# Attention, softplus layer and bilinear layer on one core: four entries of a hand-written order changed

## The chip, the core and the metric

The kernel runs as one program on one core of a Trainium2 chip. The metric is the device time of one execution in microseconds (us); the number that counts is the median of several executions. Within the core, TensorE (PE) multiplies matrices, VectorE (DVE), ScalarE (ACT) and GpSimd (POOL) work element by element, and SyncE (SP) issues the DMA transfers. Each engine works through a queue of its own, in order.

## The reference

The reference chains three parts over 3072 tokens of width 512, all in float32.

```
# 1: attention in chunks of 32 queries; each sees 56 keys around it and 8 memory keys
scores = scale * q_c @ k_full.T ; a = softmax(scores) ; x = a @ v_full
# 2: 512 -> 2048 -> 512
h = x @ w_in ;  g = maximum(h, 0) + log1p(exp(-abs(h))) ;  x = g @ w_out
# 3: 512 -> 1536 -> 512
out = ((x @ w_a) * (x @ w_b)) @ w_out2
```

## The kernel before

Tokens are cut into 8 tiles of 384 (`t` = 0 to 7). Products keep nearly full float32 precision: each operand is split into a rounded high part and a low part (names ending in `h` and `l`, or index 0 and 1), and three matmuls (high times high, high times low, low times high) are summed in PSUM.

**First phase.** For every tile and each of 16 feature blocks `f`, `emit_h` runs 12 matmuls into `ph` (L538), `emit_soft` computes the softplus (ACT: three passes over `e`, L544 to L546; DVE: `g`, L548; ACT rounds `g` to its high part, L525; POOL, or DVE in tile 0 and the last, makes the low part, L528), and `emit_x1` runs 12 matmuls into `px` (L561), two blocks later than the `ph` they come from. At a tile's end four `xo` copies (L569) go out to `x1_scratch` (L570).

**Attention in between.** Attention comes in units of 128 queries, three to a tile, and is worked on while the tile before it is in the first phase. A list `plan` of (slot, step) sets the place of each step; a slot is a half-step, two to each `f`, so `att_at(slot)` is called twice per block. A unit's steps are: turn keys and queries (L410 to L415), scores (matmuls `sc`, L302 to L305 or L429), softmax (L379, L383), normalise (L387 to L390), flip (transpose the weights into `af`), values (matmuls `pxa`, L476, which need `af`), and place (ACT casts the high part of `x`, L483; DVE makes the low part, L484). For the first units, worked on during tile 0, the flip is done on TensorE: `flip_p` runs 8 transposes `pa` (L465) and ACT copies them to `af` (L466). Their slots stand in `EARLY_STEPS`. From tile 1 on DVE does the flip, in two times five transposes (L447). The matmuls `sc`, `pxa` and `pa` share one pair of PSUM banks (tag "att").

**Weights.** In tile 0 the weights of the first phase are still being turned from 64-bit words into two floats: ACT `top` (L116), DVE `value` (L121, L122), ACT `high` (L127), DVE `low` (L130). During tiles 1 to 6 the weights of the last phase get the first half of this treatment (class `Early`): a fetch into `raw` (L625, L628, on SP), `top` on ACT (L635), `value` on DVE (L639, L640) and a store of `val` (L643, on SP). Five weights to a tile; `PRE_BY` is their distance in half-steps and `PRE_STEPS` the offset of the four steps. The fetch of one weight goes into the buffer that the weight before it leaves, so it waits for that weight's L640.

**Last phase.** Tokens are worked on in four pairs of tiles (`p`), with 12 feature blocks each. `pair_step` runs seven sums of six matmuls with 384 columns (L725), multiplies the results on DVE into `c` and splits `c` again (high: L807, L817 on ACT; low: L818 and, deferred through `pair_step.late`, L819 on DVE). After every second block six output jobs are queued; a `job` is six matmuls of 512 columns into `py` (L748), an addition to `y` on DVE (L757) and, in the last group, the transfer of `y` to the output (L760). Three jobs are taken out within each `pair_step`, and what is left is run after the last.

The program is recorded under a manual schedule: in tile 0 and from tile 7 on all engines follow the recorded order, in tiles 1 to 6 SP, PE and DVE do.

Of the kernel before, what the change touches and what calls it, by code (L numbers as in the profile page):

```python
# [23 lines left out]
TURN_LATER = ((STEPS[0][0] + 0.5, "turn"),) + STEPS[1:]  # L24
SETS = 1
EARLY_STEPS = (((4.9, "scores"), (5, "weigh"), (9, "flip_p"), (10.9, "values"), (11, "place")),
               ((12.9, "scores"), (13, "weigh"), (18, "flip_p"), (19.9, "values"), (20, "place")),
               ((20.9, "scores"), (21, "weigh"), (26, "flip_p"), (27.9, "values"), (28, "place")))
EARLY = len(EARLY_STEPS)
NEXT_LATER = 1.5  # L30
# [12 lines left out]
OUT_TAGS = "eegg"  # L43

PRE, PRE_BY = 5, 4.2
PRE_STEPS = (0, 3.4, 4.1, 4.3)
GROUP = 2


# [1 line left out]
def attn_moe_moe2(ctx: ExitStack, tc: tile.TileContext, q, k, v, mem_k, mem_v,  # L51
                  w_in, w_out, w_a, w_b, w_o2, out):
    nc = tc.nc
    B, H, S, D = q.shape
    M = mem_k.shape[2]
    NT, DM = out.shape
    F1 = w_in.shape[1]
    F2 = w_a.shape[1]
    P = 128
# [9 lines left out]
    NTILE = NT // TT  # L69
    KT = DM // P  # L70
    NF1 = F1 // P
    NF2 = F2 // P
# [446 lines left out]
    acc = {}  # L519
# [199 lines left out]
    def product(bank, p, f, n, first_):  # L719
        i, j = PLACE[n]  # L720
        u, x = us[p, f][i], sums[p, n]
        m = 0
        for kt in range(KH):
            for a, c in ((0, 0), (0, 1), (1, 0)):
                nc.tensor.matmul(bank[:, :TT], lhsT=u[:, j, a, kt * P:kt * P + P], rhs=x[:, c, kt, :],  # L725
                                 start=first_ and m == 0, stop=m == 3 * KH - 1, skip_group_check=True)
                m += 1

    def bank(tag, name):
        return ps.tile([P, 512], F32, tag=tag, name=name, bufs=1 if tag.startswith("acc") else 2)  # L730

    def temp(tag, name):
        return mp.tile([P, TT], F32, tag=tag, name=name, bufs=3 if tag in ("gh", "gl") else 2)

    cs, yacc, jobs, n_jobs = {}, {}, [], [0]
    tt = nc.vector.tensor_tensor

    def job(p, m, half, i):

        b = bank(f"acc{1 + n_jobs[0] % 3}", f"py{p}_{m}_{half}{i}")  # L740
        n_jobs[0] += 1
        fs = range(GROUP * m, GROUP * m + GROUP)
        n = 0
        for f in fs:
            c, w = cs[p, f, half], w2o[p, f]
            r = slice(i * P, i * P + P)
            for x, y in ((0, 0), (0, 1), (1, 0)):
                nc.tensor.matmul(b, lhsT=c[:, x, r], rhs=w[:, y], start=n == 0, stop=n == 3 * GROUP - 1)  # L748
                n += 1
        place = 3 * (1 - half) + i  # L750
        if m == 0:
            if place % 2 == 0:
                yacc[p, place // 2] = wp.tile([P, 2, 512], F32, tag="w", name=f"y{p}_{place // 2}")
            nc.scalar.copy(yacc[p, place // 2][:, place % 2], b)
        else:
            y = yacc[p, place // 2][:, place % 2]
            tt(y, b, y, ALU.add)  # L757
            if m == NF2 // GROUP - 1:
                r0 = (2 * p + half) * TT + i * P
                nc.sync.dma_start(out[r0:r0 + P, :], y)  # L760

    def next_job():
        if jobs:
            job(*jobs.pop(0))

    def pair_step(p, f, at, between=()):

        late_lo = pair_step.late
        x = bank("h", f"pX{p}_{f}")
        product(x, p, f, "11", True)  # L770
        s = temp("e", f"s{p}_{f}")
        nc.scalar.copy(s, x[:, :TT])
        at(0)
        y = bank("att", f"pY{p}_{f}")
        product(y, p, f, "s2", True)
        q = temp("gh", f"q{p}_{f}")
        tt(q, y[:, :TT], s, ALU.add)
        while late_lo:
            late_lo.pop(0)()
        at(1)  # L780
        if between:
            between[0]()
        else:
            next_job()
        w = bank("att", f"pW{p}_{f}")
        product(w, p, f, "s3", True)
        r = temp("e", f"r{p}_{f}")
        tt(r, w[:, :TT], q, ALU.add)
        at(2)
        if between:  # L790
            between[1]()
        v = bank("acc0", f"pV{p}_{f}")
        product(v, p, f, "s1", True)
        d22 = temp("gl", f"d22_{p}_{f}")
        tt(d22, v[:, :TT], r, ALU.add)
        at(3)
        if not between:
            next_job()
        product(x, p, f, "12", False)
        at(4)  # L800
        product(w, p, f, "22", False)
        d21 = temp("e", f"d21_{p}_{f}")
        tt(d21, w[:, :TT], q, ALU.add)  # L803
        c2 = temp("gl", f"c2_{p}_{f}")
        tt(c2, d21, d22, ALU.mult)  # L805
        cs[p, f, 1] = cc = wp.tile([P, 2, TT], F32R, tag="w", name=f"c{p}_{f}_1")
        nc.scalar.copy(cc[:, 0], c2)  # L807
        at(5)
        if not between:
            next_job()  # L810
        product(v, p, f, "s4", False)
        d12 = temp("g", f"d12_{p}_{f}")
        tt(d12, v[:, :TT], q, ALU.add)
        c1 = temp("g", f"c1_{p}_{f}")
        tt(c1, x[:, :TT], d12, ALU.mult)  # L815
        cs[p, f, 0] = c = wp.tile([P, 2, TT], F32R, tag="w", name=f"c{p}_{f}_0")
        nc.scalar.copy(c[:, 0], c1)  # L817
        tt(cc[:, 1], c2, cc[:, 0].bitcast(F32), ALU.subtract)  # L818
        late_lo.append(lambda: tt(c[:, 1], c1, c[:, 0].bitcast(F32), ALU.subtract))  # L819
        at(6)  # L820
        if f % GROUP == GROUP - 1:
            jobs.extend((p, f // GROUP, half, i) for half in (1, 0) for i in range(TT // P))
# [3 lines left out]
    def order():  # L826
# [29 lines left out]
        for i in range(BPT + 4):  # L856
            for d, step in ROUND:
                warm(FILL.get((i, step), 0))
                if d is None:
                    n = i - (step == "low")  # L860
# [29 lines left out]
        for n, e in enumerate(pre[:n_pre]):  # L890
            t, i = divmod(n, PRE)
            for d, step in zip(PRE_STEPS, (e.fetch, e.top, e.value, e.store)):
                plan.append((2 * NF1 * (t + 1) + PRE_BY * i + d, 100 + n, step))
# [56 lines left out]
        for p in range(NTILE // 2):  # L950
            more = p + 1 < NTILE // 2
            for f in range(NF2):

                def at(k):
# [22 lines left out]
                    if more:  # L977
# [8 lines left out]
                        if f == NF2 - 1:  # L986
                            if k < 5:
                                split_hi(p + 1, PRODUCTS[k], nc.scalar.copy)
                            if 0 < k < 6:
                                split_lo(p + 1, PRODUCTS[k - 1], nc.gpsimd if k in (2, 4) else nc.vector)  # L990

                pair_step(p, f, at, (between_0, between_0) if (p, f) == (0, 0) else ())
        while jobs:
            if len(jobs) == 3 and pair_step.late:
                pair_step.late.pop()()
            next_job()

    order()


# [28 lines left out]
```

## Time and profile before

| what | before |
|---|---|
| median of 3 executions | 1196.25 us (1195.96 to 1202.92) |
| the profiled execution | 1196.18 us, of which its span is 1194.1 us |
| TensorE busy | 1180.2 us, 99% of the span |
| ScalarE, VectorE, GpSimd busy | 536.3, 736.9 and 279.3 us |
| mean granted TensorE clock | 0.998 of full speed |

The span reaches from the first to the last instruction; the 2.1 us between it and the execution's time lie outside the trace. TensorE's busy time includes matmuls that run at a lower clock, so idle time and granted clock have to be read together.

### The profile page before, as it was taken

How to read it: one execution, taken by the hardware profiler on the slowest of the kernel's cores; microseconds unless marked ns; L12 is line 12 of the kernel's file. 1: busy time of each engine (PE TensorE's matmuls, PEld its weight loads, DVE VectorE, ACT ScalarE, POOL GpSimd, SP SyncE). 2: the span in 40 equal slices, each digit the busy share in tenths (PEclk: the TensorE clock that was granted, in tenths of full speed). 3: DMA queues.
4: the chain of work that ended last, by engine and by line, in shares of the span. 5: the costliest groups of instructions: out<-in, count | busy, mean ns of one | idle time of the engine just before them, and what ended most of it. 6: DMA issues, size and time to landing. Idle time of an engine off the chain costs nothing.

```text
span 1194.1 us, 21573 instructions
## 1 busy us (share of the span) xinstructions
PE 1180.2 (99%) x7994; PEld 1120.6 (94%) x7994; DVE 736.9 (62%) x1706; ACT 536.3 (45%) x1329; POOL 279.3 (23%) x249
## 2 busy tenths in 40 slices
PE   8999999999999999999999999999999999999998
PEld 8899999999999999999999999999999999999997
DVE  7888654556545565455387677755656456655565
ACT  6898656665566666566564433211112211212110
POOL 1000322323223222232325878200211002100000
PEclk9999999999999999999999999999999999999999
DMA  9955244352443534432465895788554965379521
GB/s 238 300 168 107 81 109 101 108 102 86 109 97 111 102 92 103 111 95 66 149 231 208 324 342 199 267 316 308 202 197 142 373 232 182 129 265 364 185 77 54
DMA packets 198697, 209.86 MB, mean 176 GB/s; under 512 B 121616, under 2 KB 149952, under 8 KB 198592
## 3 DMA queue, kind: packets, MB, share of 16 engines
q1 hardware_dynamic: 198208, 208.43, 54.7%
q8 instruction: 63, 1.03, 0.4%
q14 instruction: 42, 0.34, 0.1%
q0 software_dynamic: 384, 0.05, 0.0%
HBM read 158.11 MB, written 50.33 MB: 175 GB/s over the span
## 4 chain that ended last, share of the span: by engine, by line
PE 89%; DVE 3%; ACT 3%; DMA 2%; SPq 1%; issue 1%; DVEq 0%; ACTq 0%
PE ph L538 20%; PE px L561 20%; PE py L748 17%; PE pW L725 8%; PE pV L725 8%; PE pX L725 8%; PE pY L725 4%; PE pxa L476 2%; PE sc L429 1%; DMA kp<-in_k_dram 1%; DVE af L447 1%; DMA raw<-in_moe_w_in_dram 1%; ACT sm L383 1%; SPq L330 1%; DVE g L548 1%
## 5 line engine op out<-in xcount | busy, mean ns | idle before, releaser
L538 PE MATMUL ph<-x,w 128*128 128x384 f32 x1536 | 289.7, 336 | 0.1
L538 PEld LDWEIGHTS ph<-x,w 128*128 128x128 f32 x1536 | 267.0, 188 | 2.4 <-issue 0.3
L748 PE MATMUL py<-w2o,c 128*128 128x512 f32 x864 | 222.9, 394 | 0.7 <-DVE c L818 0.5
L548 DVE SCALAR_TENSOR_TENSOR g<-ph,e 128x384 f32<-128x384 f32 x128 | 71.3, 557 | 206.7 <-ACT e L546 198.8
L748 PEld LDWEIGHTS py<-w2o,c 128*128 128x128 f32 x864 | 159.9, 188 | 26.8 <-DVE c L818 1.1
L807 ACT CAST c<-c 128x384 fp32r<-128x384 f32 x48 | 24.7, 514 | 303.9 <-DVE c L805 271.2
L725 PE MATMUL pX<-x,u 128*128 128x384 f32 x576 | 115.5, 334 | 0.0
L757 DVE TENSOR_TENSOR y<-py,y 128x512 f32<-128x512 f32 x120 | 82.9, 691 | 48.2 <-PE py L748 47.8
L544 ACT ACTIVATE e<-ph 128x384 f32<-128x384 f32 x128 | 62.3, 486 | 102.3 <-PE ph L538 86.5
L725 PEld LDWEIGHTS pX<-x,u 128*128 128x128 f32 x576 | 102.1, 188 | 4.1
L447 DVE STREAM_TRANSPOSE af<-sm 32x256 f32<-32x256 f32 x180 | 78.2, 435 | 2.6
L545 ACT ACTIVATE e<-e 128x384 f32<-128x384 f32 x128 | 67.3, 526 | 4.0
L803 DVE TENSOR_TENSOR d<-pW,q 128x384 f32<-128x384 f32 x48 | 26.7, 557 | 68.4 <-PE pW L725 68.4
L546 ACT ACTIVATE e<-e 128x384 f32<-128x384 f32 x128 | 67.3, 526 | 3.7
L383 ACT ACTIVATE sm<-sm,st 128x96 f32<-128x96 f32 x168 | 60.5, 361 | 4.9 <-DVE st L379 4.9
L817 ACT CAST c<-c 128x384 fp32r<-128x384 f32 x48 | 24.6, 513 | 77.8 <-DVE c L815 76.9
L725 PE MATMUL pW<-xs,u 128*128 128x384 f32 x288 | 57.8, 335 | 0.0
L725 PE MATMUL pV<-xx,u 128*128 128x384 f32 x288 | 57.8, 335 | 0.0
L725 PE MATMUL pW<-xx,u 128*128 128x384 f32 x288 | 57.6, 334 | 0.0
L725 PE MATMUL pY<-xs,u 128*128 128x384 f32 x288 | 57.6, 334 | 0.0
L725 PE MATMUL pV<-xs,u 128*128 128x384 f32 x288 | 57.6, 334 | 0.0
L725 PEld LDWEIGHTS pV<-xx,u 128*128 128x128 f32 x288 | 51.5, 188 | 4.1
(251 smaller groups left out, 2240.0 us busy)
## 6 DMA issues: line engine op xcount, KB each, us to landing
u<-u_scratch SPq DMA_DIRECT2D x108, 512.0 KB
u_scratch<-u SPq DMA_DIRECT2D x36, 512.0 KB
w2o<-w2o_scratch SPq DMA_DIRECT2D x36, 512.0 KB
u<-u_scratch SPq DMA_DIRECT2D x36, 256.0 KB
raw<-in_moe_w_in_dram SPq DMA_DIRECT2D x16, 512.0 KB
raw<-in_moe_w_out_dram SPq DMA_DIRECT2D x16, 512.0 KB
vn<-in_v_dram SPq DMA_DIRECT2D x35, 176.0 KB
raw_a<-in_moe_w_a_dram SPq DMA_DIRECT2D x12, 512.0 KB
```

What stands on the lines that cost most here:

```text
L383: nc.scalar.activation(sm[:, h], sm[:, h], AF.Exp, bias=st[:, 0, h:h + 1], scale=-1.0, accum_out=st[:, 1, h:h + 1])
L447: nc.vector.transpose(out=af[32 * kb:32 * kb + 32, x], in_=self.sm[32 * x:32 * x + 32, :, 32 * kb:32 * kb + 32])
L538: nc.tensor.matmul(ph, lhsT=a, rhs=c, start=n == 0, stop=n == 3 * KT - 1)
L544: nc.scalar.activation(e, ph, AF.Abs)
L545: nc.scalar.activation(e, e, AF.Exp, scale=-1.0)
L546: nc.scalar.activation(e, e, AF.Ln, bias=1.0)
L548: nc.vector.scalar_tensor_tensor(g, ph, 0.0, e, ALU.max, ALU.add)
L561: nc.tensor.matmul(acc[t][i][:, :TT], lhsT=a, rhs=c, start=f == 0 and m == 0, stop=f == NF1 - 1 and m == 2)
L725: nc.tensor.matmul(bank[:, :TT], lhsT=u[:, j, a, kt * P:kt * P + P], rhs=x[:, c, kt, :], start=first_ and m == 0, stop=m == 3 * KH - 1, sk ...
L748: nc.tensor.matmul(b, lhsT=c[:, x, r], rhs=w[:, y], start=n == 0, stop=n == 3 * GROUP - 1)
L757: tt(y, b, y, ALU.add)
L803: tt(d21, w[:, :TT], q, ALU.add)
```

## The change

Four things change. The second entry of `EARLY_STEPS` has `flip_p` in slot 17 instead of 18. `PRE_STEPS` puts the steps `value` and `store` of the last phase's weights 0.9 half-steps later. In the last `pair_step` of all no job is taken out between the sums `pY` and `pW`, so that seven jobs instead of six are left for the end, and the deferred L819 is recorded when five are left instead of three. The very last job is run as two jobs of 256 columns each, with a bank, an addition and a transfer of its own for each.

```
 EARLY_STEPS = (...
-               ((12.9, "scores"), (13, "weigh"), (18, "flip_p"), (19.9, "values"), (20, "place")),
+               ((12.9, "scores"), (13, "weigh"), (17, "flip_p"), (19.9, "values"), (20, "place")),
-PRE_STEPS = (0, 3.4, 4.1, 4.3)
+PRE_STEPS = (0, 3.4, 5, 5.2)
...
-    def job(p, m, half, i):
+    def job(p, m, half, i, cols=slice(0, DM)):
...
-                nc.tensor.matmul(b, lhsT=c[:, x, r], rhs=w[:, y], start=n == 0, stop=n == 3 * GROUP - 1)
+                nc.tensor.matmul(b, lhsT=c[:, x, r], rhs=w[:, y, cols], start=n == 0, stop=n == 3 * GROUP - 1)
...
-                nc.sync.dma_start(out[r0:r0 + P, :], y)
+                nc.sync.dma_start(out[r0:r0 + P, cols], y)
...
-        else:
+        elif (p, f) != (NTILE // 2 - 1, NF2 - 1):
             next_job()
         w = bank("att", f"pW{p}_{f}")
...
         while jobs:
-            if len(jobs) == 3 and pair_step.late:
+            if len(jobs) == 5 and pair_step.late:
                 pair_step.late.pop()()
-            next_job()
+            if len(jobs) == 1:
+                last = jobs.pop()
+                job(*last, cols=slice(0, DM // 2))
+                job(*last, cols=slice(DM // 2, DM))
+            else:
+                next_job()
```

Three places show how the order moves. The first is ScalarE in tile 0, around block 9 of the first phase; `pa_4` are the TensorE transposes of the unit in question, and `raw`, `tmp`, `w` the weights of the first phase. Before:

```order
L116 ACTIVATE raw_1215<-raw_1215 128x512
L544 ACTIVATE e_9_1320<-ph_9_1301 128x384
L545 ACTIVATE e_9_1320<-e_9_1320 128x384
L546 ACTIVATE e_9_1320<-e_9_1320 128x384
L127 CAST w_1326<-tmp_1283 128x512
L525 CAST g_9h<-g_9_1324 128x384
L116 ACTIVATE raw_1217<-raw_1217 128x512
L466 COPY af<-pa_4_1337 96x4x128
L466 COPY af<-pa_4_1343 96x4x128
```

After:

```order
L466 COPY af<-pa_4_1301 96x4x128
L466 COPY af<-pa_4_1307 96x4x128
L116 ACTIVATE raw_1215<-raw_1215 128x512
L544 ACTIVATE e_9_1332<-ph_9_1313 128x384
L545 ACTIVATE e_9_1332<-e_9_1332 128x384
L546 ACTIVATE e_9_1332<-e_9_1332 128x384
L127 CAST w_1338<-tmp_1283 128x512
L525 CAST g_9h<-g_9_1336 128x384
L116 ACTIVATE raw_1217<-raw_1217 128x512
```

The two copies to `af` now stand ahead of block 9's softplus instead of behind it; the rows that follow them (w, `e_10`, raw, `g_10h`, w, and the cast of `x` from `pxa`, L483) are the same as before. On TensorE the 8 transposes stand ahead of `ph_9` instead of behind it, and nothing else moves there in tile 0.

The second place is VectorE early in tile 3, blocks 2 and 3; `af<-sm` are the flips, five transposes each, and `val_b` is a weight of the last phase.

```order
 L548 SCALAR_TENSOR_TENSOR g_2_3697<-ph_2_3680,e_2_3693 128x384
-L639 TENSOR_SCALAR val_b_3720<-raw_b_3598 128x512
-L640 SCALAR_TENSOR_TENSOR val_b_3720<-raw_b_3598,val_b_3720 128x512
 L447 STREAM_TRANSPOSE af<-sm_3612 32x256 x5
-L548 SCALAR_TENSOR_TENSOR g_3_3748<-ph_3_3731,e_3_3744 128x384
+L639 TENSOR_SCALAR val_b_3727<-raw_b_3598 128x512
+L640 SCALAR_TENSOR_TENSOR val_b_3727<-raw_b_3598,val_b_3727 128x512
+L548 SCALAR_TENSOR_TENSOR g_3_3747<-ph_3_3730,e_3_3743 128x384
 L447 STREAM_TRANSPOSE af<-sm_3612 32x256 x5
```

The two instructions of `val_b` now stand behind the first five transposes. The same happens at the start of tile 6 (and in tiles 2, 4 and 5 at this block). In tile 1, block 5, the pair instead moves from ahead of `g_5` to between `g_5` and the low part of `x` (L484).

The third place is TensorE in the last `pair_step` and behind it; `pX`, `pW`, `pV` are its sums, `py_4` and `py_5` jobs of the last two groups. Before:

```order
L748 MATMUL py_4_02_12912<-w2o_8_12500,c_8_0_12634 128x512 x3
L748 MATMUL py_4_02_12912<-w2o_9_12602,c_9_0_12736 128x512 x3
L725 MATMUL pV_11_12877<-xx_11407,u_11_3_12790 128x384 x6
L748 MATMUL py_5_10_12933<-w2o_10_12704,c_10_1_12818 128x512 x3
L748 MATMUL py_5_10_12933<-w2o_11_12806,c_11_1_12910 128x512 x3
```

After:

```order
L748 MATMUL py_4_01_0_12904<-w2o_8_12500,c_8_0_12634 128x512 x3
L748 MATMUL py_4_01_0_12904<-w2o_9_12602,c_9_0_12736 128x512 x3
L725 MATMUL pV_11_12869<-xx_11407,u_11_3_12790 128x384 x6
L748 MATMUL py_4_02_0_12925<-w2o_8_12500,c_8_0_12634 128x512 x3
L748 MATMUL py_4_02_0_12925<-w2o_9_12602,c_9_0_12736 128x512 x3
L748 MATMUL py_5_10_0_12933<-w2o_10_12704,c_10_1_12818 128x512 x3
L748 MATMUL py_5_10_0_12933<-w2o_11_12806,c_11_1_12902 128x512 x3
```

One job that needs nothing from the last block, `py_4_02`, now stands between the last sum `pV` and the first job that needs the last block's `c`. On VectorE L819 now stands behind the addition of the first `py_5` job instead of the third.

## Rows read from the trace of the kernel before

**Rows 1.** The profile's first part: busy us, share of the span, instructions.

```profile
PE 1180.2 (99%) x7994; PEld 1120.6 (94%) x7994; DVE 736.9 (62%) x1706; ACT 536.3 (45%) x1329; POOL 279.3 (23%) x249
```

**Rows 2.** Waits of TensorE, whole span: total us, times, longest.

```profile
PE pxa L476 <- DVE af L447: 1.6, 2, 1.1
```

**Rows 3.** Timeline of tile 0: start, us, engine, line; idle before, and its end.

```profile
87.92 2.25 PE L538 MATMUL ph<-x,w 128*128 128x384 f32 x12
...
89.91 0.51 ACT L525 CAST g_9h<-g 128x384 fp32r<-128x384 f32 x1 [0.42 <-DVE g L548]
...
90.89 1.04 ACT L466 COPY af<-pa 96x512 f32<-96x512 f32 x2
...
91.50 0.33 PE L476 MATMUL pxa<-af,vn 96*64 96x64 f32 x2 [1.34 <-ACT af L466]
...
93.06 0.49 PE L561 MATMUL px<-g_8h,w 128*128 128x384 f32 x1
...
95.53 0.58 ACT L483 CAST x<-pxa 128x512 fp32r<-128x512 f32 x1
...
96.67 0.68 DVE L484 TENSOR_TENSOR x<-pxa,x 128x512 fp32r<-128x512 f32 x1
...
96.91 0.29 PE L304 MATMUL sc<-kn,qn 64*64 64x88 f32 x1
...
97.41 0.29 PE L304 MATMUL sc<-kn,qn 64*64 64x88 f32 x1
```

**Rows 4.** Windows of tile 0: PE, PEld, DVE, ACT, POOL busy, granted clock, DMA.

```profile
93.00:93.50 0.50, 0.50 (x6) 0.44 (x3) 0.18 (x1) 0.47 (x2) 0.00 (x0) 0.82 0.00 0
...
96.50:97.00 0.50, 0.50 (x4) 0.17 (x5) 0.50 (x2) 0.18 (x1) 0.00 (x0) 0.77 0.90 288
```

**Rows 5.** Timeline of tile 1, blocks 5 and 6, three engines.

```profile
147.53 0.53 ACT L546 ACTIVATE e<-e 128x384 f32<-128x384 f32 x1
...
148.26 0.69 DVE L640 SCALAR_TENSOR_TENSOR val_b<-raw_b,val_b 128x512 uint32<-128x512 uint32 x1
148.86 0.55 DVE L548 SCALAR_TENSOR_TENSOR g<-ph,e 128x384 f32<-128x384 f32 x1
149.33 0.68 DVE L484 TENSOR_TENSOR x<-pxa,x 128x512 fp32r<-128x512 f32 x1
...
150.07 0.88 PE L429 MATMUL sc<-kt,qt 64*64 64x96 f32 x28 [0.55 <-DVE x L484]
```

**Rows 6.** Timeline of tile 3, blocks 2 and 3.

```profile
286.30 0.56 DVE L548 SCALAR_TENSOR_TENSOR g<-ph,e 128x384 f32<-128x384 f32 x1 [3.20 <-ACT e L546]
...
288.06 1.05 DVE L640 SCALAR_TENSOR_TENSOR val_b<-raw_b,val_b 128x512 uint32<-128x512 uint32 x1 [0.87 <-ACT raw_b L635]
...
294.16 0.69 PE L476 MATMUL pxa<-af,vn 96*64 96x64 f32 x16 [1.13 <-DVE af L447]
```

**Rows 7.** Timeline of the end: TensorE and the last addition.

```profile
1182.31 7.73 PE L748 MATMUL py<-w2o,c 128*128 128x512 f32 x31 [0.55 <-DVE c L818]
...
1190.08 0.69 DVE L757 TENSOR_TENSOR y<-py,y 128x512 f32<-128x512 f32 x1 [0.67 <-PE py L748]
```

**Rows 8.** Chain that ended last, near the end: start, us, what.

```profile
1177.13 1.04 PE pW L725 x6
1178.17 1.39 PE py L748 x6
```

**Rows 9.** Window at the last output transfer; the last column is GB/s.

```profile
1191.75:1192.00 0.25, 0.00 (x0) 0.00 (x0) 0.00 (x0) 0.00 (x0) 0.00 (x0) 1.00 1.00 385
```

**Rows 10.** Timelines of SP and ACT: fetches of raw weights, and their `top`.

```profile
140.20 0.38 SPq L628 DMA_DIRECT2D raw_b<-in_moe_w_b_dram  x1
...
144.36 0.67 ACT L635 ACTIVATE raw_b<-raw_b 128x512 f32<-128x512 f32 x1
...
289.13 0.33 SPq L625 DMA_DIRECT2D raw_o<-in_moe_w_out_dram  x1
...
295.15 0.68 ACT L635 ACTIVATE raw_o<-raw_o 128x512 f32<-128x512 f32 x1
```

More of the change, by code (lines that the diff above doesn't have):

```diff
@@ L736, in attn_moe_moe2 @@
     tt = nc.vector.tensor_tensor
-    def job(p, m, half, i):
-        b = bank(f"acc{1 + n_jobs[0] % 3}", f"py{p}_{m}_{half}{i}")
+    def job(p, m, half, i, cols=slice(0, DM)):
+        b = bank(f"acc{1 + n_jobs[0] % 3}", f"py{p}_{m}_{half}{i}_{cols.start}")[:, cols]
         n_jobs[0] += 1
@@ L755, in job @@
         else:
-            y = yacc[p, place // 2][:, place % 2]
+            y = yacc[p, place // 2][:, place % 2, cols]
             tt(y, b, y, ALU.add)
```

## The prediction

> **What bounds the kernel now.** I read the parts in this order: busy times, TensorE's waits, then the timelines around each wait. TensorE is busy 1180.2 us of a span of 1194.1 [rows 1], so an edit of the order can win back only part of 13.9 us of idle time, plus what TensorE loses at a lower clock. The list of waits then says where the change can reach: `pxa` waits for the flips on VectorE 1.6 us in all, in two places, the longer one 1.1 [rows 2], so the other is 0.5. The timelines add three more places: `pxa` in tile 0 behind the copies to `af` (1.34 us), `sc` in tile 1 behind the low part of `x` (0.55 us) and the first `py_5` job behind L818 (0.55 us) [rows 3, 5, 7]. Everywhere else in the stretches that the change touches TensorE goes from one block to the next without a gap, so an edit there costs or gains nothing unless it makes a new wait. The clock is the last thing to read: in tile 0 it falls to half inside the window from 93.00 and is back inside the window from 96.50. Shares of 0.82 and 0.77 put the ends at 93.32 and 96.73 [rows 4], so the stretch is 3.4 us long.
>
> **Tile 0, the flip a half-step sooner.** On TensorE the 8 transposes and `ph_9` change places, so `ph_10` still ends at 90.2 (87.92 + 2.25 [rows 3]). `pxa` then finds its `af` copied and starts at once, at about 90.0 instead of 91.50: the wait of 1.34 us goes. The block behind it also runs at full clock, so that TensorE has done `pxa` (1.1 us) and `px` of block 8 (12 matmuls at 173 ns, from 1.04 us for six [rows 8]: 2.1 us) by 93.1, where before it had them at 96.91. Next come the scores of the following unit. Some 0.4 us of them have a bank that is free; the others cannot start before `x` is read out of the shared banks by L484 at 96.67; before, they restarted at 97.41, 0.06 us after it ended [rows 3]. So what decides is when L484 comes, and that is set by ScalarE: L483, on which L484 waits, stands in ScalarE's queue behind block 10's softplus.
>
> How much sooner can L483 come? Between 89.91 and 95.53 ScalarE works through the same instructions as before, less the two copies (1.04 us), but those now stand ahead of `e_9` and push it back. VectorE's `g_9` then waits for `e_9` about 0.65 us longer (it started at about 89.32, as soon as VectorE was free, with `e_9` ready some 0.3 us earlier; `e_9` now comes 0.95 later), and the cast `g_9h`, at 89.91 before, starts at 90.56. From there the missing copies give back 0.95 (the distance at which the next instruction followed them): 0.3 us sooner in all. The bounds: nothing, if everything is pushed back by as much as the copies take; 0.42, the one idle time of ScalarE in front of `g_9h` [rows 3]. I take 0.3, so the scores restart at 97.1 and TensorE stands idle from 93.5 to 97.1, 3.6 us in one piece where it had 1.34 and about 0.1 before.
>
> Now the clock. Before, TensorE fell idle at 90.2, and the clock fell at 93.3, after 1.34 us of idle time and 1.1 us of the small `pxa` matmuls; most of the half-clock stretch lay on `px` of block 8, whose 12 matmuls took 3.85 us instead of 2.08 (from 93.06 to the first scores at 96.91 [rows 3]). That cost nothing, because the scores could start no sooner than L484 allowed. After the change the longer idle time should make the clock fall again, and this time the matmuls behind the wait pay, with nothing to hide them: behind the scores TensorE goes on for tens of microseconds without a wait that could take them up. If the clock falls 3.1 us after the idle time starts, as before, at 96.2, and is back 3.4 us later at 99.6, then 2.5 us of the stretch lie behind 97.1 and cost half of that, 1.2 us. Bounds: 0 (the whole stretch inside the wait) and 1.7 (all 3.4 us behind it). I take 1.2, as the one whose timing a row shows. Sum for tile 0: -0.3 + 1.2 = **+0.9 us**, bounds -0.4 to +1.7.
>
> The Trainium skill, page "TensorE: Matmul & The Clock Gate", section "Why this matters for your kernels", speaks against this edit: it advises against idle gaps between matmul bursts, since the clock goes back to half rate after one. By it the fall is sure and the sum stands; were there none, tile 0 would be -0.3 and the whole 1193.4. The trace has a fall after 1.34 us of idle time in tile 0 and none at the 1.13 us in tile 3.
>
> **VectorE's part of the weights later.** It adds and removes no instruction, only moves L639 and L640, together about 1.1 us.
> - Tile 3. Before, `g` (286.30), L640 (0.87 us of idle time for `top`, then 1.05 us), five transposes, `g`, five transposes, `pxa` [rows 6]. After, the first five transposes fill the time in which VectorE waited for `top`, and the second five end 0.87 us sooner or more, since L640 took 1.05 here and 0.69 where GpSimd was idle [rows 5, 6]: 0.36 more. That is 1.2 against a wait of 1.13. I take **-1.1**, bounds -0.9 and -1.13.
> - Tile 6 has the same rows and a wait of 0.5 [rows 2]: **-0.5**; bounds -0.5 and -0.3, if only part of it was due to the weight.
> - Tile 1. Here the pair moves from ahead of `g_5` to between `g_5` and L484, for which `sc` waits 0.55 us [rows 5]. The two used to run while ScalarE was still on `e_5`; `g_5` can start only when L546 ends, at 148.06, where VectorE, without L639 (0.42) ahead of 148.26, is free at 147.8. So 0.3 us is lost on VectorE in front of L484 and `sc` starts that much later. GpSimd's low part of `g_5` also starts sooner and will overlap L640, which may cost up to the 0.36 of above. **+0.6**, bounds 0 and +0.9.
> - The Trainium skill, page "Advanced Engine Details and Errata", section "GPSIMD Details", says that GpSimd shares a read and a write interface with VectorE and conflicts with its instructions that have two SBUF inputs. L640 has two; by this rule tile 1 would be +0.65, without a conflict +0.3. The trace agrees so far as L640 took 1.05 beside GpSimd's work and 0.69 beside none.
> - Elsewhere the pair moves behind softmax or flips, of which no one waits on L640 but the next fetch (a rival, below). The stores on SP now stand behind eight of the key and query loads, which is a gain for the loads. Cost nothing.
>
> **The end.** The kept job (1.39 us [rows 8]) now covers the wait for L818 (0.55 us [rows 7]), since L818 and what leads to it come 1.39 sooner against the jobs. At the second `py_5` half the 31 matmuls take 7.73 us, where 31 at 232 ns (1.39 / 6) are 7.19: some 0.3 of the 0.54 is lost to the late L819, the rest is the last matmul draining. L819 now comes two additions earlier, 1.4 us, which covers it. The `y` addition behind the kept job goes to VectorE ahead of L819, where there is room. Both together: **-1.0 us**, bounds -0.85 and -1.3.
>
> The last job in halves: no row shows a 256-column matmul. Half of a 512-column one is 116 ns, and it should not take more than the 384-column one, 173. Twelve cost 1.39 to 2.08 us against 1.39 for the six: between 0 and +0.7. I take 120 ns, +0.05, since both longer shapes go by 0.45 ns a column. Behind the last matmul the addition has half the columns (0.69 to about 0.42, from the 0.56 for 384 and 0.69 for 512: -0.27), and the last transfer half of 256 KB, at 385 GB/s [rows 9] 0.34 us less. **-0.55**, bounds -0.6 and +0.1.
>
> **Sum.** +0.9 - 1.1 - 0.5 + 0.6 - 1.0 - 0.55 = -1.65 us, on an execution of 1196.18, which is the median (1196.25) to 0.1 us: **1194.6 us**. With all lower ends it is 1192.5, with all upper ends 1196.9.
>
> **Rivals.** (1) *The clock costs more than all else wins.* The wait in front of the scores is 2.7 times the one before; if the half-clock stretch comes twice in a row (6.8 us, all behind 97.1), tile 0 costs -0.3 + 3.4 = +3.1, and the sum is +0.55: 1196.8, slower than before. It decides from 5.8 us of half clock behind the wait (2.9 us, what the rest wins). For it: the long idle time. Against it: the one fall that the trace shows ended after 3.4 us. (2) *The clock stays up, or its low stretch lies inside the wait.* Then tile 0 gains 0.3, sum -2.85: 1193.4. For it: much of the stretch may fall into 3.6 us of wait. (3) *The weights' transfers come late.* The next fetch waits for L640, which moves by up to 1.7 us (tile 3). There the fetch left at 289.13 and its `top` ran at 295.15; a fetch is known to land within 4.2 us (140.20 to 144.36, where `top` waited for nothing) [rows 10]. After the change the distance is 6.0 - 1.7 - 1.1 = 3.2, so ScalarE may be held up to 1.0 us in front of its softplus. If two tiles pass that on to TensorE, +2.0: 1196.6. Against it: a block's `g` is needed only two blocks later.
>
> **Chances.** The forecast 0.55, rival 1 0.13, rival 2 0.2, rival 3 0.07, others 0.05. The range takes in rivals and bounds, 1192.0 to 1198.6; its upper end leaves 1.7 us above the worst sum because one of the three executions shown lies 6.7 us above the other two. A measurement of this kernel tells a change from none at about 1%, 12 us; no case comes near that, so faster 0.02, same 0.96, slower 0.02.
>
> **What would show it.** Right: no wait of `pxa` for the copies, a wait of some 3.6 us at `sc` L304 behind L484 near 97, a stretch at half clock that starts near it and covers scores and `ph_11`; `pxa` without a wait in tiles 3 and 6; a wait of 0.9 to 1.2 at `sc` in tile 1; the jobs' matmuls at the end without a gap. Wrong: L484 more than half a microsecond sooner, no fall of the clock, a wait of ScalarE for `raw`, or 256-column matmuls at 170 ns.

## The result and the profile after

The changed kernel is slower: 1215.63 us median of six executions (1213.49 to 1218.22) against 1197.66 of six of the kernel before (1195.96 to 1202.92), a ratio of 1.0143 with a 95% interval of 1.0116 to 1.017. That is 17 to 18 us more, where 1.65 us of gain was forecast.

The profiled execution has a span of 1215.4 us, 21.3 us above that of before. Two views show where TensorE spends them. First the page's busy times, then the list of TensorE's waits (total us, times, longest), both of the changed kernel; [rows 1, 2] are the same of before.

```profile
PE 1191.2 (98%) x8000; PEld 1131.8 (93%) x8000; DVE 739.8 (61%) x1707; ACT 538.5 (44%) x1329; POOL 282.8 (23%) x249
```

```profile
PE pxa L476 <- DVE af L447: 11.9, 7, 2.3
PE sc L304 <- DVE x L484: 3.2, 1, 3.2
PE sc L429 <- DVE x L484: 1.9, 3, 0.9
```

Idle time grew from 13.9 to 24.2 us, and busy time by 11.0 us although no more was added than six matmuls (twelve of half width stand for six): the second is a lower clock, in the mean 0.987 of full speed against 0.998. The wait that was to shrink, `pxa` for the flips, went from 1.6 us in two places to 11.9 in seven. To see in which stage the time goes, the next table counts from the first `xo` copy (L569) of one tile to that of the next, in us; its cells are differences of start times read in the two timelines, and of the spans' ends (1194.08 and 1215.44 us).

| stretch | before | after | difference |
|---|---|---|---|
| start to the first `ph` (L538) | 37.41 | 41.87 | +4.5 |
| first `ph` to the first `xo`: tile 0 | 94.24 | 96.18 | +1.9 |
| tile 1 | 74.94 | 77.82 | +2.9 |
| tile 2 | 73.87 | 76.26 | +2.4 |
| tile 3 | 75.72 | 78.37 | +2.7 |
| tile 4 | 73.92 | 77.26 | +3.3 |
| tile 5 | 73.87 | 75.87 | +2.0 |
| tile 6 | 73.62 | 76.90 | +3.3 |
| tile 7 to its first `xo` | 62.87 | 62.86 | 0.0 |
| from there to the end | 553.62 | 552.06 | -1.6 |

The 4.5 us ahead of the first `ph` are not the change's: nothing is moved there, and that stretch took from 37.6 to 42.1 us in the executions of the experiments below. What differs is the clock, which in this execution was at half from 18.4 to 32.1 us. The window around it, in the changed kernel and in the one before (us busy of PE, PEld, DVE, ACT, POOL with counts; granted clock; DMA share; GB/s):

```profile
18.00:33.00 15.00, 15.00 (x147) 13.40 (x145) 10.42 (x45) 11.34 (x39) 0.00 (x0) 0.54 0.99 254
18.00:33.00 15.00, 12.68 (x193) 11.04 (x192) 13.86 (x59) 13.63 (x51) 0.00 (x0) 1.00 1.01 252
```

What is left is 16.5 us in tiles 1 to 6, that is in the weights' part, which the prediction had at -1.0; 1.9 in tile 0 (predicted +0.9); and -1.6 at the end (predicted -1.55).

**One tile closely.** The chain of work through tile 1, in the changed kernel (start, us, what; "issue" is time that waits for nothing that the profile shows):

```profile
168.67 0.40 DVE val_o L639
169.07 0.02 issue
169.10 1.85 DVE val_o L640
170.95 0.02 SPq L628
170.97 0.04 issue
171.01 3.91 DMA raw_a<-in_moe_w_a_dram
174.93 0.02 issue
174.95 0.67 ACT raw_a L635
175.61 0.42 ACT e L546
...
176.12 0.56 DVE g L548
176.68 0.03 issue
176.71 0.04 DVE af L447
```

And the timelines of GpSimd, ScalarE and TensorE there (start, us, engine and line; in brackets the idle time before and what ended it):

```profile
168.90 1.49 POOL L390 TENSOR_TENSOR sm<-sm,st 128x768 f32<-128x768 f32 x1 [4.96 <-ACT e L544]
170.35 1.46 POOL L528 TENSOR_TENSOR g_7l<-g,g_7h 128x384 fp32r<-128x384 f32 x1
...
174.95 0.67 ACT L635 ACTIVATE raw_a<-raw_a 128x512 f32<-128x512 f32 x1 [1.39 <-DMA raw_a<-in_moe_w_a_dram]
...
179.00 0.69 PE L476 MATMUL pxa<-af,vn 96*64 96x64 f32 x16 [1.75 <-DVE af L447]
```

The same place in the kernel before, of which the prediction shows no row (timelines of VectorE, SP and ScalarE; this kernel runs 6.74 us earlier here, by the `g` that starts at 161.14 before and at 167.88 after):

```profile
157.59 0.69 DVE L640 SCALAR_TENSOR_TENSOR val_o<-raw_o,val_o 128x512 uint32<-128x512 uint32 x1
161.14 0.56 DVE L548 SCALAR_TENSOR_TENSOR g<-ph,e 128x384 f32<-128x384 f32 x1 [2.86 <-ACT e L546]
...
168.07 2.24 DVE L447 STREAM_TRANSPOSE af<-sm 32x256 f32<-32x256 f32 x5
...
158.31 0.40 SPq L628 DMA_DIRECT2D raw_a<-in_moe_w_a_dram  x1
...
164.60 0.66 ACT L635 ACTIVATE raw_a<-raw_a 128x512 f32<-128x512 f32 x1
165.77 0.49 ACT L544 ACTIVATE e<-ph 128x384 f32<-128x384 f32 x1 [0.51 <-PE ph L538]
...
166.85 0.53 ACT L546 ACTIVATE e<-e 128x384 f32<-128x384 f32 x1
```

Read downwards: `val_o` is the third of the tile's five weights. Its L640 stood ahead of `g` and the normalise step and now stands behind both: it starts 4.8 us later (169.10 against 157.59 + 6.74) and takes 1.84 us instead of 0.69, while GpSimd's L390 and then L528 run beside it. The fetch of the fourth weight waits for it and leaves 6.0 us later (171.01 against 165.05). The transfer takes 3.9 us, so its `top` can run at 174.95; before, it ran 6.3 us after its fetch left, which means 2.4 us in hand. ScalarE's queue has that `top` between the second and the third pass of softplus `e_9`. So L546 ends 1.9 us late, `g` behind it starts late too, and `g` stands in VectorE's queue ahead of the second five transposes, on which `pxa` waits. Every tile from 1 to 6 has this wait once, of 1.75, 1.58, 1.78, 1.89, 2.06 and 2.28 us.

The place of `top` is not the same in all six. ScalarE does not follow the recorded order in these tiles. In the kernel before, `top` stands ahead of all three passes of `e_9`; in the changed kernel it stands between the second and the third in tiles 1 to 3, and ahead of all three in tiles 4 to 6, where it holds ScalarE for 2.84, 2.85 and 3.11 us. Tile 4:

```profile
404.54 0.67 ACT L635 ACTIVATE raw_a<-raw_a 128x512 f32<-128x512 f32 x1 [2.84 <-DMA raw_a<-in_moe_w_a_dram]
405.11 0.47 ACT L544 ACTIVATE e<-ph 128x384 f32<-128x384 f32 x1
```

**The clock behind the waits.** Windows of the changed kernel, as above:

```profile
330.00:335.00 5.00, 3.22 (x38) 2.93 (x38) 4.85 (x11) 2.87 (x7) 1.00 (x1) 0.74 0.08 21
335.00:340.00 5.00, 5.00 (x54) 4.63 (x54) 1.21 (x3) 1.18 (x2) 1.01 (x1) 0.91 0.95 215
410.00:415.00 5.00, 5.00 (x32) 4.93 (x27) 3.36 (x7) 1.62 (x5) 1.01 (x1) 0.66 0.59 165
560.00:565.00 5.00, 2.72 (x39) 2.28 (x38) 4.53 (x10) 2.75 (x6) 1.00 (x1) 0.96 0.01 3
565.00:570.00 5.00, 5.00 (x32) 4.75 (x34) 1.91 (x4) 1.65 (x5) 1.01 (x1) 0.70 0.82 227
```

Behind three of the six waits TensorE ran at half clock for a time. These shares miss 5 x (0.26 + 0.09 + 0.34 + 0.04 + 0.30) = 5.2 us of full speed. With 10.3 us more of waits at `pxa` and 1.4 more at `sc` L429 that makes 16.9, against the 16.5 of the table.

**Tile 0** went as the prediction described it, with rival 1's size. The timeline and two windows:

```profile
101.06 0.40 PE L304 MATMUL sc<-kn,qn 64*64 64x88 f32 x1 [3.21 <-DVE x L484]
```

```profile
100.00:100.50 0.50, 0.00 (x0) 0.00 (x0) 0.50 (x2) 0.33 (x1) 0.00 (x0) 0.84 0.94 345
...
107.00:107.50 0.50, 0.50 (x4) 0.50 (x3) 0.50 (x1) 0.12 (x1) 0.00 (x0) 0.83 0.14 19
```

The wait for `af` is gone and 3.21 us at `sc` stand in its place (3.6 predicted). The clock fell at 100.34 (a mean of 0.84 means that 0.16 of the window's 0.5 us were at half clock) and came back at 107.17 (0.83, so 0.17 us of it): 6.8 us at half clock, of which 6.1 lie behind the start of the scores.

**The end** (VectorE's last additions, [rows 7] of before):

```profile
1209.23 0.69 DVE L757 TENSOR_TENSOR y<-py,y 128x512 f32<-128x512 f32 x1 [0.67 <-PE py L748]
1210.60 1.14 DVE L757 TENSOR_TENSOR y<-py,y 128x512 f32<-128x512 f32 x2 [0.67 <-PE py L748]
1212.03 0.42 DVE L757 TENSOR_TENSOR y<-py,y 128x256 f32<-128x256 f32 x1 [0.29 <-PE py L748]
```

No job waits for L818 any more, the last addition takes 0.42 us, and from its end to the span's it is 2.99 us where it was 3.31.

### The profile page after: what moved, and what is told of

Read it like the earlier page. It is cut to its first block, busy times and chain, and to the rows that moved or that the text cites. A ratio compares the mean times of both kernels' runs of the same rounds, so it can differ in the third digit from the quotient of the medians.

```text
span 1215.4 us, 21576 instructions
## 1 busy us (share of the span) xinstructions
PE 1191.2 (98%) x8000; PEld 1131.8 (93%) x8000; DVE 739.8 (61%) x1707; ACT 538.5 (44%) x1329; POOL 282.8 (23%) x249
## 3 DMA queue, kind: packets, MB, share of 16 engines
q8 instruction: 63, 1.03, 0.4%
## 4 chain that ended last, share of the span: by engine, by line
PE 82%; ACT 7%; DVE 6%; DMA 3%; issue 1%; SPq 0%; DVEq 0%; ACTq 0%
PE py L748 16%; PE ph L538 16%; PE px L561 15%; PE pW L725 8%; PE pV L725 8%; PE pX L725 8%; PE pY L725 4%; ACT sm L383 2%; PE pxa L476 1%; DVE g L548 1%; ACT e L546 1%; DVE af L447 1%; ACT e L545 1%; PE sc L429 1%; DMA raw_b<-in_moe_w_b_dram 1%
## 5 line engine op out<-in xcount | busy, mean ns | idle before, releaser
L538 PE MATMUL ph<-x,w 128*128 128x384 f32 x1536 | 292.2, 338 | 0.1
L538 PEld LDWEIGHTS ph<-x,w 128*128 128x128 f32 x1536 | 269.4, 189 | 2.4 <-issue 0.3
L748 PE MATMUL py<-w2o,c 128*128 128x512 f32 (+1 forms) x870 | 222.5, 392 | 0.0
L757 DVE TENSOR_TENSOR y<-py,y 128x512 f32<-128x512 f32 (+1 forms) x121 | 83.0, 686 | 46.0 <-PE py L748 45.5
L546 ACT ACTIVATE e<-e 128x384 f32<-128x384 f32 x128 | 67.3, 526 | 3.8
```

The costliest lines, as they stand in the source:

```text
L538: nc.tensor.matmul(ph, lhsT=a, rhs=c, start=n == 0, stop=n == 3 * KT - 1)
L546: nc.scalar.activation(e, e, AF.Ln, bias=1.0)
L748: nc.tensor.matmul(b, lhsT=c[:, x, r], rhs=w[:, y, cols], start=n == 0, stop=n == 3 * GROUP - 1)
```

## Experiments

**The theory** (T): the third weight's late L640 delays the fourth weight's transfer, which holds ScalarE inside a softplus, and through `g` the flips. **Rivals**: (V) the work itself, slowed by GpSimd to 1.84 us just ahead of the flips, delays them; (T2) the lateness adds up over all five weights; (F) the early flip in tile 0 puts the later tiles out of step.

Ratios are to the kernel before, run beside each group of four kernels, with 95% intervals; its median was 1199.66 us beside the first four, 1198.22 beside the next four and 1198.57 beside the last four.

### The parts, each alone

Four kernels made from the one before. The first has the change's `PRE_STEPS`, the second its `EARLY_STEPS`, the third its new `job`, `pair_step` and last loop:

```
-PRE_STEPS = (0, 3.4, 4.1, 4.3)
+PRE_STEPS = (0, 3.4, 5, 5.2)
...
-               ((12.9, "scores"), (13, "weigh"), (18, "flip_p"), (19.9, "values"), (20, "place")),
+               ((12.9, "scores"), (13, "weigh"), (17, "flip_p"), (19.9, "values"), (20, "place")),
...
-            next_job()
+            if len(jobs) == 1:
+                last = jobs.pop()
+                job(*last, cols=slice(0, DM // 2))
+                job(*last, cols=slice(DM // 2, DM))
+            else:
+                next_job()
```

The fourth has the new `PRE_STEPS` for one weight of five:

```
-            for d, step in zip(PRE_STEPS, (e.fetch, e.top, e.value, e.store)):
+            steps = PRE_STEPS if i == 2 else (0, 3.4, 4.1, 4.3)
+            for d, step in zip(steps, (e.fetch, e.top, e.value, e.store)):
```

Weights alone: 

> The kernel before with PRE_STEPS alone changed. Theory T (late transfer: the third weight of a tile is finished later, so the fetch of the fourth leaves later, ScalarE is held by it in the middle of a softplus, the g behind it stands in VectorE's queue ahead of the second five transposes, pxa waits, and the clock falls after the wait): it carries the six tiles' 16.5 us of the changed kernel's trace, so +14 to +18 us against before, with a wait of pxa for L447 of 1.5 to 2.3 us in each of tiles 1 to 6. Rival F (the early flip in tile 0 starts it, by pushing the later tiles out of step): under +4 us here. My prediction's term for this part alone was -1.0.

Flip alone: 

> The kernel before with flip_p in slot 17 alone. From the changed kernel's trace tile 0 loses 2.6 us: a wait of sc at L304 for L484 of 3.2 us, then 6 to 7 us at half clock of which some 6 lie behind the wait. Theory C (clock behind the wait): +2.5 us (2.0 to 3.1), nothing in the other tiles. Rival F: +10 us and more, the other tiles suffer too. The prediction's term was +0.9.

End alone: 

> The kernel before with the end's two changes alone (kept job, last job in halves). By the changed kernel's trace -1.6 us (-1.3 to -1.9), by the prediction -1.55: no wait of py for L818, last addition 0.42 us, a shorter last transfer. A rival, that the halves cost as much as the kept job wins: 0.

Third weight alone: 

> The kernel before with value and store moved later for the third of each tile's five weights alone. Theory T: this one move makes the fetch of the fourth weight late, so most of the loss of all five is here: +11 to +17 us, pxa waits for L447 in tiles 1 to 6. A rival T2, that the lateness of the weights adds up over the five (each late one makes the next later): the third alone would cost under +6 us.

| kernel | median | ratio |
|---|---|---|
| weights alone | 1215.84 | 1.0129 (1.0108 to 1.015) |
| flip alone | 1200.23 | 1.0011 (0.9997 to 1.0026) |
| end alone | 1197.25 | 0.9978 (0.9963 to 0.9992) |
| third weight alone | 1214.23 | 1.0115 (1.0089 to 1.014) |

The weights' part carries the loss, and of its five weights the third by itself carries it: F and T2 fall. TensorE's waits with the third weight alone:

```profile
PE pxa L476 <- DVE af L447: 13.6, 7, 2.0
```

One of the seven is the wait of tile 3 that the whole change shortens ([rows 6]); it stays when the first weight is not moved (2.01 us here). The flip alone is at the edge of what can be told (+1.3 us, -0.4 to +3.1). The end gives 2.6 us (1.0 to 4.4).

### Is it the transfer, or VectorE's own work?

The first kernel leaves L639 and L640 of the third weight where they were and adds the same two operations, on other data, where the change puts them:

```
+        def again(self):
+            d = mp.tile([P, 512], U32, tag="tmp", name=f"again_{self.name}", bufs=2)
+            nc.vector.tensor_scalar(d, self.val, 29, None, ALU.logical_shift_right)
+            nc.vector.scalar_tensor_tensor(d, self.val, 3, d, ALU.logical_shift_left, ALU.bitwise_or)
...
+            if i == 2:
+                plan.append((2 * NF1 * (t + 1) + PRE_BY * i + 5, 100 + n, e.again))
```

The second has the weights' change and moves the fourth weight's `top`:

```
-            for d, step in zip(PRE_STEPS, (e.fetch, e.top, e.value, e.store)):
+            steps = (0, 4.9, 5, 5.2) if i == 3 else PRE_STEPS
+            for d, step in zip(steps, (e.fetch, e.top, e.value, e.store)):
```

The third has the weights' change with the third weight left where it was:

```
+            steps = PRE_STEPS if i != 2 else (0, 3.4, 4.1, 4.3)
```

> The kernel before with the third weight's L639 and L640 left in their old place and two instructions of the same size added in the place to which the change moves them (behind the normalise step, ahead of the flips); their result is not used. VectorE so has the changed kernel's load at that place, and the fetch of the fourth weight leaves as early as before. Theory T (late fetch holds ScalarE): the loss does not appear; the flips start 0.5 us later, the wait of pxa stays under 0.6 us per tile, 0 to +3 us in all. Rival V (the work itself, slowed by GpSimd beside it to 1.84 us, delays the flips): pxa waits 1.5 to 2 us in each of six tiles, +11 us or more.

> The kernel before with the weights' change, but the top of the fourth weight of each tile placed 1.5 half-steps later, so that in ScalarE's queue it stands behind the softplus e_9 and the cast g_9h instead of in the middle of e_9. Transfer, L640 and VectorE's order stay those of the weights' change. Theory T: e_9 no longer waits for the transfer, so g_9 and the second five transposes are on time: -9 us or more against the weights' change alone, that is 0 to +5 us against before. Rival V: as the weights' change alone, +15 us.

> The kernel before with the weights' change for four of each tile's five weights, the third left where it was. Theory T: the waits in the middle of e_9 go, and what the move of the first weight wins in tiles 3 and 6 stays: -2 to +1 us against before, no wait of pxa over 0.6 us. Rival T2 (lateness adds up over the weights): +6 us or more.

| kernel | median | ratio |
|---|---|---|
| same work, fetch as early as before | 1199.17 | 1.0003 (0.9992 to 1.0014) |
| weights' change, `top` behind the softplus | 1198.71 | 1.0005 (0.9992 to 1.0018) |
| weights' change without the third | 1198.24 | 0.9995 (0.998 to 1.0011) |

V falls with the first line. VectorE had the whole load there, at the slow rate, and the flips followed on it (VectorE's timeline, tile 1):

```profile
163.79 1.84 DVE L645 SCALAR_TENSOR_TENSOR again_o<-val_o,again_o 128x512 uint32<-128x512 uint32 x1
...
166.03 2.22 DVE L447 STREAM_TRANSPOSE af<-sm 32x256 f32<-32x256 f32 x5
```

Yet `pxa` waited only 0.33 us in that tile, and 1.0 us over all in the places of that kind:

```profile
172.29 0.69 PE L476 MATMUL pxa<-af,vn 96*64 96x64 f32 x16 [0.33 <-DVE af L447]
```

The second line is the sharper one: L640 late, beside GpSimd, and the fetch and the stores as late as in the weights' change alone. Only `top` stands further on in ScalarE's queue, behind L546 and `g_9h`, and the loss is gone, with no wait of `pxa` for the flips left in the list. ScalarE still waits for a late transfer, the fifth weight's, but at a place where the softplus behind it has to wait for its `ph` anyway (its timeline, tile 1):

```profile
171.28 0.51 ACT L525 CAST g_9h<-g 128x384 fp32r<-128x384 f32 x1 [0.69 <-DVE g L548]
171.70 0.68 ACT L635 ACTIVATE raw_a<-raw_a 128x512 f32<-128x512 f32 x1
...
179.03 0.67 ACT L635 ACTIVATE raw_b<-raw_b 128x512 f32<-128x512 f32 x1 [1.73 <-DMA raw_b<-in_moe_w_b_dram]
180.63 0.49 ACT L544 ACTIVATE e<-ph 128x384 f32<-128x384 f32 x1 [0.94 <-PE ph L538]
```

So a late transfer that holds ScalarE for 1.7 us at one place of its queue costs nothing, and one that holds it for 1.2 to 3.1 us at another costs 2 to 3 us in each tile.

### What sets tile 0, and the pieces of the end

In one more kernel the unit's `values` and `place` go a half-step sooner with its flip:

```
-               ((12.9, "scores"), (13, "weigh"), (18, "flip_p"), (19.9, "values"), (20, "place")),
+               ((12.9, "scores"), (13, "weigh"), (17, "flip_p"), (18.9, "values"), (19, "place")),
```

> The kernel before with flip_p in slot 17 and also values and place of that unit one half-step sooner (18.9 and 19), so that L483 and L484 stand ahead of block 10's softplus and g. If what decides in tile 0 is when L484 comes, the wait of sc at L304 goes, no half-clock stretch follows it, and tile 0 is 1.5 to 3 us shorter than with the flip alone: -1 to 0 us against before. If tile 0's low clock comes from something else than that wait, it stays as with the flip alone, +1 to +2 us.

1197.89 us, ratio 0.9995 (0.9982 to 1.0009); the flip alone had 1.0011. The wait at `sc` L304 is gone and TensorE stays at full clock between 88 and 108 us, so L484's time was what decided. But another takes its place: the next early unit's `pxa` waits 1.70 us for `af` at 112, and the clock is at half for 6.8 us from 112.7 on.

The two pieces of the end, each alone, are read from the stretch between the first `xo` of tile 7 and the end of the span, 553.62 us before, in one execution of each. The first kernel has the left-out job and the earlier L819, the second the halves:

```
+        elif (p, f) != (NTILE // 2 - 1, NF2 - 1):
+            if len(jobs) == 5 and pair_step.late:
```

```
+                job(*last, cols=slice(0, DM // 2))
+                job(*last, cols=slice(DM // 2, DM))
```

> The kernel before with the kept job at the end alone (L819 when five are left, the last job whole). From the start of the last sum pV to the last instruction: before 14.70 us plus the job that stood ahead of it. The prediction's term is -1.0 (bounds -0.85 to -1.3): no wait of py for L818. Read from the stretch behind the last pX of the trace, since it is below what executions tell.

> The kernel before with the last job in two column halves alone. The prediction's term is -0.55 (bounds -0.6 to +0.1): 256-column matmuls of about 120 ns, last addition 0.42 instead of 0.69 us, last transfer 0.34 us shorter. If a 256-column matmul costs as much as one of 384 columns (173 ns), the halves take 0.7 us more on TensorE and the sum is +0.1.

552.51 with the kept job (-1.1) and 553.08 with the halves (-0.5); end alone (both) 551.82 (-1.8). In the changed kernel's trace the matmuls of 256 columns start 120 ns apart (the second at 1210.51 us, the last, ten later, at 1211.71), as was estimated.

### A version that wins

Both kernels have the changes at the end and the first two lines here; the second has the new `PRE_STEPS` for the first weight of each tile as well:

```
+               ((12.9, "scores"), (13, "weigh"), (17, "flip_p"), (18.9, "values"), (19, "place")),
+               ((20.9, "scores"), (21, "weigh"), (25, "flip_p"), (26.9, "values"), (27, "place")))
...
+            steps = PRE_STEPS if i == 0 else (0, 3.4, 4.1, 4.3)
```

> The kernel before with the end's two changes, with the second early unit's flip_p, values and place in slots 17, 18.9 and 19, and the third early unit's in 25, 26.9 and 27 (before 26, 27.9, 28). By the traces: the end gives -1.6 us, the wait of pxa for the copies to af (1.3 to 1.7 us with the clock's fall behind it) goes in both units: -2.5 to -4 us against before. A rival, that the wait of 1.7 us near 112 only moves on to the next step of tile 0: -1.5 us.

> As the kernel with both early units sooner and the end's changes, and the weights' change for the first of each tile's five weights alone. If the first weight's move does what the prediction said of tiles 3 and 6, their waits of pxa (about 1.1 to 1.5 and 0.5 us) go and nothing else appears: -1.0 to -1.6 us further, -4 to -5.5 us against before. If the fetch of the second weight, which then leaves later, holds ScalarE in a softplus as the fourth's does: +1 us or more in each tile where it does, slower than the kernel with both units sooner.

| kernel | median | ratio |
|---|---|---|
| end, both units sooner | 1192.72 | 0.9953 (0.9935 to 0.9972) |
| and the first weight later | 1190.62 | 0.9929 (0.9906 to 0.9952) |

Both win more than expected: the wait did not move on, and no other appeared behind it in tile 0. The second's trace does lose some 3 us earlier in tile 0, at a wait of 2.19 us with half clock behind it, but both kernels have the same code there, and the first waits 0.64 us:

```profile
48.91 1.27 PE L293 MATMUL ptq<-ident,qp 128*64 128x128 f32 x12 [2.19 <-DVE qn L295]
```

With the second, `pxa` has all but stopped waiting for the flips:

```profile
PE pxa L476 <- DVE af L447: 0.2, 1, 0.2
```

Its tiles 1 to 6 are 2.3 us shorter than the first one's, 1.2 of it in tile 3 (73.99 against 75.23) and 0.6 in tile 6 (73.43 against 74.06). It is the fastest of all kernels here, 8 us below the one before and 25 below the changed one; that the first weight's part of it counts rests on one trace of each, since the two intervals overlap.

## Why the prediction was wrong, point by point

**The step that failed** is in the part on the weights: "Elsewhere the pair moves behind softmax or flips, of which no one waits on L640 but the next fetch", at a cost of nothing, together with rival 3, which named the right chain (fetch, transfer, `top`, softplus) and gave it a chance of 0.07 and 2.0 us. It rested on two sentences. One was that L640 "moves by up to 1.7 us (tile 3)". That is the shift of the first weight. The steps of the plan are called only at whole half-steps, so 0.9 of one moves the others a whole slot, and what lies in that slot differs from weight to weight: for the third it is a `g` and the normalise step, with GpSimd at work beside it, and L640 starts 4.8 us later. The other was "a block's `g` is needed only two blocks later". That is true of `px`, but `g` also stands in VectorE's queue, in front of the second five transposes, and those are needed at once. The fourth weight's transfer had 2.4 us in hand and was put off by 6.0. The rows for that sum were in the trace of before; [rows 10] showed it for one weight, and the argument took that one for all. The prediction did name "a wait of ScalarE for `raw`" as a sign of being wrong, and that is what came.

**The clock** made it a half worse: 5.2 of the 16.5 us. The Trainium skill, page "TensorE: Matmul & The Clock Gate", section "Why this matters for your kernels", advises against idle gaps between matmul bursts. The runs agree in part: at the waits of 1.78, 1.89 and 2.28 us the clock fell, at those of 1.58, 1.75 and 2.06 us it did not.

**Tile 0** (+0.9, bounds -0.4 to +1.7): measured +1.9 against this execution, beyond the bounds, and +1.3 (-0.4 to +3.1) by the times of the flip alone. The mechanism was right: L484 came 0.31 us sooner, counted from the start of `ph_10` (87.92 and 91.88), where 0.3 was forecast. The term was mis-sized: the half-clock stretch was 6.8 us, not 3.4. What the prediction could not see from one trace is that the tile varies as much without the change. From `ph_10` to the first `xo`, the unmoved flip took 43.7 us in four traces, that of before among them, 45.2 to 45.3 in four, and 46.9 in the kernel with the weights alone, 44.7 in the mean; the moved flip took 46.2 in the changed kernel and 46.3 alone. That is 2.4 us more than in the trace of before and 1.5 more than the mean. The end-alone kernel has the same wait of 1.31 us, but its clock held on until the scores:

```profile
98.00:99.00 1.00, 0.17 (x8) 0.18 (x10) 0.77 (x2) 0.09 (x1) 0.00 (x0) 1.00 0.76 292
99.00:100.00 1.00, 1.00 (x35) 1.00 (x32) 0.00 (x0) 0.00 (x0) 0.00 (x0) 0.58 1.01 387
```

and fell on matmuls that nothing hides. So the trace of before was at the favourable end, and "cost nothing, because the scores could start no sooner" held for it and for two more of the nine (the third weight alone, the kept job alone), whose clock fell on `px` of block 8 as well.

**Tiles 3, 6 and 1** (-1.1, -0.5, +0.6): right in kind, where nothing covers them. The first weight's move gave -1.2 and -0.6 in tiles 3 and 6 of the last two kernels above. But the wait of 1.13 us in tile 3 was one execution's: it lay between 0.42 and 2.01 us in the nine traces in which the first weight is not moved, and between nothing and 0.61 in the five in which it is. In tile 1 `sc` waits 0.91 us instead of 0.55, +0.4, which is the forecast without its part for GpSimd: L640 took 0.69 us there, although L528 ran beside most of it.

```profile
155.48 0.69 DVE L640 SCALAR_TENSOR_TENSOR val_b<-raw_b,val_b 128x512 uint32<-128x512 uint32 x1
...
155.74 1.29 POOL L528 TENSOR_TENSOR g_5l<-g,g_5h 128x384 fp32r<-128x384 f32 x1 [3.79 <-ACT g_5h L525]
```

GpSimd slowed L640 at a place that the prediction gave no cost, the third weight's, and by more than the 1.05 us it had read: to 1.84. The Trainium skill, page "Advanced Engine Details and Errata", section "GPSIMD Details", names this conflict; the 1.84 us agree with it, the 0.69 of tile 1 do not.

**The end** (-1.0 and -0.55): measured -1.1 and -0.5, together -1.6 in the changed kernel. All steps held.

**The sum.** The lower ends add up to -3.9, that is 1192.3 us and not 1192.5; nothing rests on it.

## What to carry to other kernels

When an instruction is moved that frees a buffer, follow the refill for every instance of it: how long before its use the transfer left, how long it takes, and which instructions stand in the waiting engine's queue behind the one that uses it. A wait on a side engine is harmless or not by its place in the queue: here 1.7 us in front of one block cost nothing, and 1.2 to 3.1 us in front of or within another 2 to 3 us. And one profiled execution shows one outcome; where a clock that rises and falls decides, read the same stretch in several traces before giving it a cost.

## What the runs showed of the hardware

- The same two-input VectorE instruction on 128x512 words (L640) took 0.69 us alone, 1.03 to 1.20 beside one L528 of GpSimd that had begun before it, and 1.84 where L390 and then L528 ran beside it from start to end, in six tiles of six. Where L528 began 0.26 us after it, as in block 5 of all six tiles of the changed kernel, it took 0.69 as well.
- The clock does not follow from the length of the wait alone. It stayed at full rate behind 1.53 us in tile 3 of the kernel with the same work and an early fetch, behind 1.75 us in tile 1 and 2.06 in tile 5 of the changed kernel, and it fell behind 1.75 us in tile 1 of the weights alone:

```profile
176.00:177.00 1.00, 0.90 (x17) 0.78 (x17) 0.94 (x3) 0.00 (x0) 0.00 (x0) 0.71 0.00 0
177.00:178.00 1.00, 1.00 (x3) 1.00 (x4) 1.00 (x3) 0.59 (x1) 0.00 (x0) 0.50 0.00 0
```

- The stretch ahead of the first `ph`, the same code in every kernel here, took 37.4 to 39.0 us in the eleven traces in which the clock is full there from 18 us on, and 40.1, 41.9 and 42.1 us in the three in which it is at half for 6.8, 13.7 and 13.7 us; what makes it fall there is not shown.
